# Scaling v of four chunks on VectorE instead of GpSimd, and taking out one group of identity products

## The chip, the cores and the metric

The kernel runs on one core of a Trainium2 chip. The metric is the device time of one execution in microseconds (us), as the median of several runs. The profile is one execution recorded by the hardware; its span, from first to last instruction, is 1.7 us shorter than the time of the same run. In its lines PE is TensorE, PEld TensorE's weight loads, DVE VectorE, ACT ScalarE, POOL GpSimd, and L168 is line 168 of the kernel. A timeline line gives start, duration, engine, line, operation, output from input, and in brackets how long the engine sat idle before it and what ended that; xN means N instructions put into one line. The granted clock is the share of its full speed that TensorE's clock had, as the profile records it.

Each run is on record with a state, fast or slow. All timed runs used below are of the fast state, but for three single runs of the kernel before, whose state is not known; from those only the traces are used.

## The reference

A retention layer (a decaying linear attention, per head h with decay gamma_h) is followed by a gated feed-forward layer:

```
state = gamma[h] * state + outer(k[t], v[t])        # t = 0..767, state 64 x 64
y[t]  = (1/sqrt(64)) * q[t] @ state
x     = y with the 8 heads side by side             # 3072 tokens x 512
out   = (sigmoid(x @ w_gate) * (x @ w_val)) @ w_out # 512 -> 1536 -> 512
```

There are 4 sequences of 768 tokens. The kernel cuts them into 24 chunks of 128 tokens, numbered 0 to 23, six per sequence.

## The kernel before

Each chunk takes these steps: load k, q, v; transpose k and q; scale v by a table of decays (`scale_v`); multiply k and q into scores and mask them; add the part that comes from the state (`inter`) and the part inside the chunk (`intra`); update the state (`state`). Four finished chunks make a tile of 512 tokens for the feed-forward part. The chunk steps of tile t + 1 are placed between the matmuls of tile t. The order of statements is the order in each engine's queue: in the trace of this kernel the last of the twelve loads that the program puts ahead of the scaling of chunk 8 ends on GpSimd at 71.05 us, and the scaling starts at 71.07. In this kernel TensorE's results go to buffers in PSUM, and what the other engines write lies in SBUF. Names in the lines: `kn`, `qn`, `vf` are the loaded k, q, v; `vs` is the scaled v; `tp` the transposes in PSUM and `qkT` their copy (`qkX` where a DMA transposes); `sA`, `sB` the scores; `z` the state; `hT` the gate times the value; `ff` a ring of three PSUM buffers; `tabv`, `taby` the tables of decays. Cuts are marked with `...`.

```python
ld  = ...tile_pool(name="ld", bufs=12)             # k, q: 12 buffers; v: 8; scaled v: 4
pf  = ...tile_pool(name="pf", bufs=3, space=PSUM)  # the ring "ff"
XBAR = 12          # chunks from 12 on are transposed by DMA, those before on TensorE

def load_chunk(g):                                 # three loads issued on GpSimd
    load_kq(g)
    load_v(g, nc.gpsimd)

def scale_v(g, eng):                               # both inputs in SBUF
    vs[g] = ld.tile([C, H, D], BF16, tag="vs", name="vs", bufs=4)
    eng.tensor_tensor(vs[g], vf[g], tabv[...], op=ALU.mult)

def step_t(g):
    if g < XBAR:
        transposes(g)                              # TensorE, then a copy qkT on ScalarE
    scale_v(g, nc.vector if g < 8 else nc.gpsimd)

def keep_on(n):                                    # identity products: results are not used
    u = pf.tile([128, 512], F32, tag="ff", name="ff")
    for _ in range(n):
        nc.tensor.matmul(u[:, :128], ident, ident, start=True, stop=True)

def extend_taby():                                 # "the table product", reads SBUF
    nc.gpsimd.tensor_tensor(taby[:, :, 384:768], taby[:, :, 0:384], ..., op=ALU.mult)
...
    load_gate_val(1); load_gate_val(2)             # weights, in six slices, on GpSimd
    ...
    extend_taby()
    for s in range(3, NFF // 2):
        load_gate_val(s)
    load_chunk(4)
...
    scale_v(3, nc.vector)
    keep_on(8)
    up(0, 0, 0, 384)                               # gate and value matmuls, sigmoid, hT
    up(0, 1, 0, 384)
    transposes(3)
    keep_on(16)
    scores(3)
    masks(3)
    inter(3)
    state(3)
...
for t in range(NT):
    ...
    if t + 2 < NT:
        for g in range(4 * t + 8, 4 * t + 12):     # t = 1: chunks 12 to 15
            load_chunk(g)
    for i, group in enumerate(groups):             # t = 1: step_t(8) to step_t(11) are in here
        group()
        ...
```

In tile 1 the loads of chunks 12 to 15 therefore stand ahead of the scaling of chunks 8 to 11 in GpSimd's queue.

## Time and profile before

| | before |
|---|---|
| time, median of 3 runs | 240.25 us (239.96 to 240.81) |
| profiled run | 239.9 us, span 238.2 us |
| TensorE busy | 229.9 us, 96% |
| TensorE's wait for GpSimd's scaling of chunk 8 | 0.88 us, at 72.18 us |
| wait before the identity products of the fourth chunk | 0.99 us, at 21.17 us |
| VectorE's scaling of v: median and longest | 684 ns, 2307 ns |

TensorE is busy in 96% of the span, and its matmuls run in the order of the program (the scores of the fourth chunk, whose data was there at 21.24 us, start at 22.16, behind the 16 products), so the way to read this kernel is to look for holes in its stream and ask what ended each. The lines are in the prediction below.

### The profile page before, as it was taken

The page shows a single profiled execution, that of the slowest core. Times are in us where ns is not written, and L with a number is a line of the kernel's source. Part 1 is how long each engine was busy: PE and PEld are TensorE (multiplying, and loading weights), DVE is VectorE, ACT ScalarE, POOL GpSimd, SP SyncE. Part 2 cuts the span into 40 slices and gives each one's busy share as a digit, 9 for nine tenths or more (in the row PEclk, how much of TensorE's full clock was granted, in tenths as well). Part 3 has the DMA queues.
Part 4 walks back from the last instruction along what each step waited for, and adds up shares of the span by engine and source line. Part 5 has one row for each costly group of instructions (what it writes and reads, how often), then busy time and mean ns, then how long its engine had stood idle before and what let it go on. Part 6 is the DMA issues. An engine that isn't in the chain of part 4 may idle for free.

```text
span 238.2 us, 4369 instructions
## 1 busy us (share of the span) xinstructions
PE 229.9 (96%) x1754; PEld 120.7 (51%) x1754; DVE 103.0 (43%) x174; ACT 90.8 (38%) x170; POOL 95.9 (40%) x114
## 2 busy tenths in 40 slices
PE   7898999999998999999999999999999999999994
PEld 7665644555654554444554445444445554444443
DVE  3557446355545532166542256641256641234300
ACT  7764334425544442234433234333233431333211
POOL 8999875687889626973411001111000000000000
PEclk9999999999999999999999999999999999999999
DMA  7999999999999999999999462002100011100022
GB/s 136 187 192 183 186 203 204 188 210 223 235 178 128 124 130 160 277 123 120 108 125 152 125 96 44 3 37 80 64 0 0 3 44 73 62 0 0 0 88 88
DMA packets 77699, 27.27 MB, mean 115 GB/s; under 512 B 65072, under 2 KB 73264, under 8 KB 77680
## 3 DMA queue, kind: packets, MB, share of 16 engines
q0 software_dynamic: 57616, 16.78, 71.8%
q1 hardware_dynamic: 19776, 10.10, 22.7%
q8 instruction: 13, 0.21, 0.4%
q10 hardware_dynamic: 288, 0.13, 0.2%
q14 instruction: 6, 0.05, 0.1%
HBM read 28.31 MB, written 6.29 MB: 145 GB/s over the span
## 4 chain that ended last, share of the span: by engine, by line
PE 87%; POOL 7%; issue 2%; DVE 1%; ACT 1%; POOLq 0%; DVEq 0%
PE ff L250 49%; PE ff L281 25%; PE sA L168 3%; PE y L204 2%; PE z L190 2%; POOL kn L67 2%; PE y L180 2%; POOL vf L62 1%; POOL qn L68 1%; POOL vs L158 1%; PE tp L146 1%; PE ff L301 1%; PE ff L264 1%; PE ff L293 1%; DVE xT L212 1%
## 5 line engine op out<-in xcount | busy, mean ns | idle before, releaser
L255 DVE TENSOR_TENSOR hT<-gs,ff 128x512 bf16<-128x512 f32 (+1 forms) x72 | 48.7, 677 | 76.0 <-PE ff L250 74.4
L250 PE MATMUL ff<-xT,wg 128*128 128x512 bf16 (+1 forms) x288 | 72.8, 375 | 0.4 <-DVE xT L212 0.3
L250 PE MATMUL ff<-xT,wv 128*128 128x512 bf16 (+1 forms) x288 | 72.6, 375 | 0.0
L254 ACT ACTIVATE gs<-ff 128x512 f32<-128x512 f32 (+1 forms) x72 | 42.3, 588 | 68.7 <-PE ff L250 68.7
L281 PE MATMUL ff<-wo,hT 128*128 128x512 bf16 x276 | 63.0, 379 | 0.0
L250 PEld LDWEIGHTS <-wv 128*128 128x128 bf16 x288 | 28.2, 98 | 32.7
L250 PEld LDWEIGHTS <-wg 128*128 128x128 bf16 x288 | 26.6, 98 | 30.2 <-issue 0.8
L281 PEld LDWEIGHTS <-hT 128*128 128x128 bf16 x276 | 25.9, 98 | 30.1
L158 POOL TENSOR_TENSOR vs<-vf,tabv 128x512 bf16<-128x512 f32 x18 | 18.6, 1048 | 44.8 <-PE y L204 39.8
L286 ACT COPY ob<-ff 128x512 f32<-128x512 f32 x23 | 13.5, 586 | 52.2 <-PE ff L281 47.0
L62 POOL DMA_DIRECT2D vf<-in_v_dram x23 | 20.7, 898 | 11.5 <-DMA kn<-in_k_dram 6.4
L212 DVE TENSOR_TENSOR xT<-y,taby 128x512 bf16<-128x512 f32 x24 | 16.4, 685 | 20.1 <-PE y L204 20.0
L173 DVE TENSOR_TENSOR stA<-sA,causal 128x512 bf16<-128x512 f32 x24 | 16.5, 687 | 18.7 <-PE sB L168 18.6
L67 POOL DMA_DIRECT2D kn<-in_k_dram x23 | 20.8, 904 | 8.0 <-DMA qn<-in_q_dram 5.7
L68 POOL DMA_DIRECT2D qn<-in_q_dram x23 | 20.4, 886 | 4.0 <-DMA wo<-in_moe_w_out_dram 2.2
L198 ACT CAST zbd<-z 64x256 bf16<-64x256 f32 x40 | 14.7, 366 | 14.5 <-PE z L190 14.1
L174 DVE TENSOR_TENSOR stB<-sB,causal 128x512 bf16<-128x512 f32 x24 | 16.3, 681 | 0.0
L148 ACT ACTIVATE qkT<-tp 128x1024 bf16<-128x1024 bf16 x12 | 12.3, 1025 | 5.1 <-PE tp L146 5.1
L293 PE MATMUL ff<-ident 128*128 128x128 bf16 x110 | 10.0, 257 | 2.6 <-POOL ident masks.py:199 1.6
L293 PEld LDWEIGHTS <-ident 128*128 128x128 bf16 x110 | 8.4, 119 | 3.2 <-POOL ident masks.py:199 1.6
L204 PE MATMUL y<-stA,vs 128*64 128x128 bf16 x96 | 9.7, 222 | 0.0
L204 PE MATMUL y<-stB,vs 128*64 128x128 bf16 x96 | 9.5, 221 | 0.0
(52 smaller groups left out, 119.7 us busy)
## 6 DMA issues: line engine op xcount, KB each, us to landing
vf<-in_v_dram POOLq DMA_DIRECT2D x23, 256.0 KB, 9.2
out_dram<-ob SPq DMA_DIRECT2D x23, 256.0 KB, 2.0
kn<-in_k_dram POOLq DMA_DIRECT2D x23, 128.0 KB, 8.9
qn<-in_q_dram POOLq DMA_DIRECT2D x23, 128.0 KB, 9.2
wg<-in_moe_w_gate_dram POOLq DMA_DIRECT2D x6, 256.0 KB, 5.9
wv<-in_moe_w_val_dram POOLq DMA_DIRECT2D x6, 256.0 KB, 6.6
wo<-in_moe_w_out_dram POOLq DMA_DIRECT2D x4, 384.0 KB, 10.7
kf<-in_k_dram SPq DMA_DIRECT2D x1, 256.0 KB, 3.3
```

What stands on the lines that cost most here:

```text
L62: eng.dma_start(out=vf[g], in_=src(v, g))
L67: nc.gpsimd.dma_start(out=kn[g], in_=src(k, g))
L68: nc.gpsimd.dma_start(out=qn[g], in_=src(q, g))
L158: eng.tensor_tensor(vs[g], vf[g], tabv[:, g % NCH, :].unsqueeze(2).to_broadcast([C, H, D]), op=ALU.mult)
L173: nc.vector.tensor_tensor(stA[g], sc[g][0], causal4, op=ALU.mult)
L204: nc.tensor.matmul(y[g][i * D:(i + 1) * D, p, :], vs[g][:, 2 * p + i, :], st[:, p, :], start=(first and p == 0), stop=True, skip_group_che ...
L212: nc.vector.tensor_tensor(xT[g // 4][:, :, col:col + C], y[g], taby[:, :, c * C:(c + 1) * C], op=ALU.mult)
L250: nc.tensor.matmul(u[:, lo:hi], w[:, kk, n1 * 128:(n1 + 1) * 128], xT[t][:, kk, lo:hi], start=(kk == 0), stop=(kk == KT - 1))
L254: nc.scalar.activation(gs[:, lo:hi], ps[0][:, lo:hi], AX.Sigmoid)
L255: nc.vector.tensor_tensor(hT[t][:, n1, lo:hi], gs[:, lo:hi], ps[1][:, lo:hi], op=ALU.mult)
L281: nc.tensor.matmul(o, hT[t][:, n1, sm * 128:(sm + 1) * 128], wo[:, n1, :], start=(n1 == 0), stop=(n1 == NFF - 1))
L293: nc.tensor.matmul(u[:, :128], ident, ident, start=True, stop=True)
```

## The change

The intent is to remove two delays of TensorE: a group of identity products, and a wait for a scaled v that stands behind twelve load issues.

```diff
     def step_t(g):
         if g < XBAR:
             transposes(g)
-        scale_v(g, nc.vector if g < 8 else nc.gpsimd)
+        scale_v(g, nc.vector if g < XBAR else nc.gpsimd)
@@
     up(0, 1, 0, 384)
     transposes(3)
-    keep_on(16)
     scores(3)
```

The parts are called A (no products) and B (VectorE scales chunks 8 to 11).

## The prediction

> **What bounds the kernel now.** I began with the page: which engine is full, and what the chain that ended last is made of.
>
> ```profile
> PE 229.9 (96%) x1754; PEld 120.7 (51%) x1754; DVE 103.0 (43%) x174; ACT 90.8 (38%) x170; POOL 95.9 (40%) x114
> ...
> PE 87%; POOL 7%; issue 2%; DVE 1%; ACT 1%; POOLq 0%; DVEq 0%
> ```
>
> TensorE (PE) is busy in 96% of a 238.2 us span and holds 87% of the chain. Whatever shortens its in-order stream, or fills a hole in it, comes off the end; work moved between other engines counts only where TensorE waits for it. GpSimd (POOL), 40% busy, holds 7% of the chain, so somewhere TensorE does wait for it. The view of waits of TensorE says how often:
>
> ```profile
> PE z L190 <- POOL vs L158: 1.2, 2, 0.9
> PE ff L293 <- DVE hT L255: 1.0, 1, 1.0
> ```
>
> These are the two waits of weight after the start. The first is one wait of 0.9 us (and one of 0.3 us near 11.7 us, which the change doesn't touch): the state matmuls of a chunk wait for a v scaled on GpSimd. The second is before identity products (line 293). I then read the timeline around each. First the products behind the fourth chunk's transposes:
>
> ```profile
> 17.27 2.82 POOL L130 TENSOR_TENSOR taby<-taby,gup 128x1536 f32<-128x1536 f32 x1
> ...
> 18.35 2.31 DVE L158 TENSOR_TENSOR vs<-vf,tabv 128x512 bf16<-128x512 f32 x1 [1.42 <-DMA vf<-in_v_dram]
> ...
> 20.22 1.02 ACT L148 ACTIVATE qkT<-tp 128x1024 bf16<-128x1024 bf16 x1 [0.61 <-PE tp L146]
> 20.58 1.00 DVE L255 TENSOR_TENSOR hT<-gs,ff 128x384 bf16<-128x384 f32 x2
> 21.17 1.05 PE L293 MATMUL ff<-ident 128*128 128x128 bf16 x16 [0.99 <-DVE hT L255]
> ```
>
> The products write into a PSUM buffer of the ring "ff" (three deep), which comes free only when VectorE has made the first hT. VectorE is late because its scaling of v took 2.31 us beside GpSimd's table product. So the products, meant to fill a hole, begin 0.99 us after TensorE ran dry and end behind it. The data that the next useful work (scores of the fourth chunk) needs was there at 20.22 + 1.02 = 21.24 us; the scores' first row in the same view starts at 22.16.
>
> Then the GpSimd wait, in the timeline of 71 us, with the next chunk's step, which has no wait, below it:
>
> ```profile
> 70.16 0.89 POOL L62 DMA_DIRECT2D vf<-in_v_dram  x1
> ...
> 70.91 0.23 PE L168 MATMUL sA<-qkT 64*128 64x128 bf16 x1
> ...
> 71.07 4.05 POOL L158 TENSOR_TENSOR vs<-vf,tabv 128x512 bf16<-128x512 f32 x4
> ...
> 72.18 0.32 PE L190 MATMUL z<-vs,kn 128*64 128x64 bf16 x8 [0.88 <-POOL vs L158]
> ...
> 78.61 0.23 PE L168 MATMUL sA<-qkT 64*128 64x128 bf16 x1
> ...
> 78.94 0.32 PE L190 MATMUL z<-vs,kn 128*64 128x64 bf16 x8
> ```
>
> GpSimd issues the twelve loads of chunks 12 to 15 before it comes to scaling v of chunk 8, because the program puts those loads ahead in its queue. The last ends at 71.05, the scaling starts at 71.07, TensorE goes on at 72.18. The time of the scaling is set by the loads' queue, not by v, which was issued at 47.18 and landed 7.9 us later, at 55.1.
>
> [...] The scaling has two SBUF inputs. [...] 684 ns in the median of its six VectorE runs, but 2307 ns beside the table product, ending at 20.66, some 0.57 us after the product's end at 20.09. [...]
>
> [...] The trace shows a granted clock of 1.00 in the stretch 20.00 to 21.20, where TensorE worked 0.21 us. No trace here shows what triggers a drop.
>
> [...] The trace says 1042 against 684 ns, a factor of 1.5[...].
>
> **The change part by part.**
>
> Part A, no identity products. It removes 16 matmuls. By duration (219 ns each) they would be 3.5 us, but they are pipelined: 21.17 to 22.16 is 0.99 us for 16, 62 ns each. After it the scores are released by the copy qkT (21.24). At 13.97 us the same step starts 0.06 us after a copy that ended at 13.91, so I put the scores at 21.30. The gain is 22.16 − 21.30 = 0.86 us, not 0.99: 0.13 us of it becomes a wait for ScalarE. The ring of ff buffers turns by one place; the next gate product then needs the first hT (done 21.13) and starts near 22.2, so nothing new binds. VectorE finishes two hT at 21.58, just before the scores can be masked, near 21.73. All that follows moves up by 0.86.
>
> Does that survive up to 71 us? The DMA share is in the nineties, so loads don't move up with TensorE. The tightest is chunk 5: its k was issued at 32.40 and its q at 33.35, both landing 11.1 us later, so 43.5 and 44.45. Its transposes load k at 45.78 and q at 46.16 now, and would at 44.92 and 45.30. That leaves 0.85 us for q. The last piece of the output weights lands near 31.07 + 11.5 = 42.6 and isn't wanted before 44.5. Chunk 6 has k at 46.7 against 48.4. All clear, if narrowly.
>
> Part B, v of chunks 8 to 11 on VectorE. It takes 4 × 1.04 us from GpSimd and adds 4 × 0.68 = 2.7 us to VectorE. For chunk 8 the scaling stands behind an hT row that ends at 61.94; v was there at 55.1, so vs is ready near 62.6 (61.8 with part A), nine us early. The state products then follow the scores as at 78.61 to 78.94, that is by 0.33 us: they would have started at 71.24 instead of 72.18. Gain 0.94 us. VectorE can carry the addition: between two hT rows it waits 1.04 us for TensorE, and one scaling fits; the others fall near 67.6, 77 and 83 us, with v landed at 59.3, 62.6 and 65.8. GpSimd computes nothing then[...].
>
> The parts depend on each other. With A alone, TensorE would arrive 0.86 us earlier at 71 us and wait 0.86 us longer for a GpSimd whose time is set by DMA. B makes A count. Together 0.86 + 0.94 = 1.80 us. After 73 us no wait of TensorE for another engine is above 0.3 us, so the sum should reach the end: 240.25 − 1.80 = 238.45 us.
>
> GpSimd becomes free 4 us earlier and can issue the loads of chunks 16 and 17 from 71 instead of 75 us. But the loads then go at the pace of landings (the rows of chunks 18 and 19 wait 2.2 and 4.2 us for earlier DMAs), so I count nothing. Its next scaling (93.94) is wanted only by 108.5.
>
> **The rivals.**
>
> First, the identity products did a service[...]. For it: they were put there to keep TensorE on. Against: the present trace already has 0.99 us of idleness there with the clock at 1.00, and the hole grows by only 0.13 us. [...] I give it 7%.
>
> Second, part A is lost to late data: TensorE would wait for q of chunk 5 or its kin, as loads stay where they are. For it: margins of 0.85 us with DMA full, and landings that move from run to run. Against: the sum of margins above. The time would be about 239.0 to 239.3. Whatever it waits for there, at least B's 0.94 remains. 12%.
>
> Third, VectorE becomes the late one[...]. For it: the 2.31 us case. Against: v is landed by nine us or more, and no GpSimd arithmetic is left between 55 and 90 us. A block of 1.6 us past a slack of 1 us would cost 0.6 us or so per case. 6%.
>
> Fourth, earlier loads crowd the transposing DMAs of chunks 12 to 15 (issued 66.67 to 83.33, some 10.7 us to land) and the output writes behind them. Against: they are wanted only at 100.83, seven us after. Worth nothing unless they slip by that much. 4%.
>
> **Range and chances.** The centre is 238.45. The three times of before spread over 0.85 us, and my two gains are each good to about 0.2 us if no rival bites. With the rivals, which lean upward, 237.8 to 239.4 should hold it 8 times in 10. Faster by over 2% would need below 235.4, three us more than all I can find; slower by over 2% needs above 245[...]. So 1%, 98%, 1%.
>
> **What would show each step.** In the changed trace: scores of the fourth chunk start near 21.3 us behind the copy qkT, and the wait of line 293 for hT is gone (A). The transposes of chunk 5 start 0.86 us earlier with no wait for a DMA (A carried); if a wait for qn stands there, the second rival is right. The scaling shows ten rows on VectorE, all but one near 684 ns, and fourteen on GpSimd; the state products near 70.4 us follow the scores by 0.33 us and GpSimd leaves the chain between 61 and 72 us (B). Granted clock 1.00 from 20 to 25 us, else the first rival. The span falls from 238.2 to about 236.4. I'd be wrong if the gain is about 0.9 (one part lost), or if a later wait on loads of chunks 12 to 19 stands in TensorE's view.

The trace of the kernel before shows this in their place. VectorE's scaling of v took 684 ns in the median of six, and 2307 ns in the one that ran beside GpSimd's table product; another (at 49.47 us) took 0.68 us beside a load issue of GpSimd from 49.00 to 49.87. The 1042 ns are GpSimd's median for the same scaling. The page's DMA row has a 9 (90% or more) in every slice from 6 to 131 us; in the first trace of the change the load of q of chunk 5 was issued at 33.56 us, against 33.35 before, although TensorE came to its transposes 0.57 us earlier. That landings move from run to run shows in four traces of the kernel before: VectorE's scaling of chunk 3, which waits for its v, started at 18.35, 18.47, 18.41 and 18.45 us. That loads set GpSimd's time at 71 us was inference.

The rivals: the first is that without the products the granted clock falls at the hole. What that would cost was not shown; its 7% was the estimate, from the hole of 0.99 us with the clock at 1.00. The third is that a scaling on VectorE comes late, as the one of 2.31 us did, and delays the hT behind it; its 1.6 us is an estimate, 2307 − 684 ns.

## The result, and the profile after

| | before | after |
|---|---|---|
| median of 4 runs, same rounds | 240.13 us | 238.13 us |
| lowest, highest | 239.96, 240.81 | 238.13, 238.38 |
| span of the profiled run | 238.2 us | 236.7 us |
| granted clock, mean | 1.000 | 0.997 |

The ratio is 0.9914, with a 95% interval of 0.9893 to 0.9935. A ratio here is the mean time of one kernel's fast runs over that of the other's fast runs of the same rounds, so it is not quite the ratio of the medians above. The difference of 2 us is clear of the noise.

The profiled run was the slowest of the four. The other three had a span of 236.4 us. Its extra 0.28 us comes from the start: the first scaling on GpSimd waited for a load of v and began at 8.35 instead of 8.08 us, the second scaling followed it, and from the state products that wait for that one (12.04 instead of 11.75 us) TensorE is later by 0.28. Its clock dips only in the last of 40 slices. A second trace of the changed kernel, taken later, has a span of 236.4 and a start like that of before; it is used beside the first.

The chain that ended last, on the page of the changed kernel. In it GpSimd had 7% before:

```profile
PE 90%; DMA 3%; ACT 2%; POOL 2%; issue 1%; DVE 1%; SPq 0%; ACTq 0%; DVEq 0%; POOLq 0%
```

The waits of TensorE in the changed kernel (total, times, longest):

```profile
PE sA L168 <- ACT qkT L148: 2.1, 4, 1.1
PE ff L293 <- POOL ident masks.py:199: 1.6, 1, 1.6
...
PE z L190 <- POOL vs L158: 0.4, 1, 0.4
```

The wait of line 293 for hT is gone, and so is the 0.88 us at 72 us (the 0.4 left is at 12 us). A wait of 1.1 us for ScalarE's copy qkT has come in; it is the old hole, now ended by the copy. The two places in the timeline of the changed kernel, first the fourth chunk:

```profile
17.54 2.83 POOL L130 TENSOR_TENSOR taby<-taby,gup 128x1536 f32<-128x1536 f32 x1
...
18.14 2.79 DVE L158 TENSOR_TENSOR vs<-vf,tabv 128x512 bf16<-128x512 f32 x1 [0.93 <-DMA vf<-in_v_dram]
...
20.50 1.02 ACT L148 ACTIVATE qkT<-tp 128x1024 bf16<-128x1024 bf16 x1 [0.61 <-PE tp L146]
20.85 1.00 DVE L255 TENSOR_TENSOR hT<-gs,ff 128x384 bf16<-128x384 f32 x2
...
21.58 0.23 PE L168 MATMUL sA<-qkT 64*128 64x128 bf16 x1 [1.12 <-ACT qkT L148]
```

The scores start at 21.58 instead of 22.16 us, 0.58 earlier in a run that was 0.28 late: 0.86 us. Then chunk 8:

```profile
61.28 0.68 DVE L158 TENSOR_TENSOR vs<-vf,tabv 128x512 bf16<-128x512 f32 x1
...
70.33 0.23 PE L168 MATMUL sA<-qkT 64*128 64x128 bf16 x1
...
70.66 0.32 PE L190 MATMUL z<-vs,kn 128*64 128x64 bf16 x8
```

The scaling is done nine us before it is needed, and the state products follow the scores by 0.33 us, as they do in steps without a wait. They start at 70.66 instead of 72.18: with the late start, 1.80 us are gained by here. In the second trace of the change,

```profile
70.39 0.32 PE L190 MATMUL z<-vs,kn 128*64 128x64 bf16 x8
```

that is 1.79 us earlier than before, and the span is 1.8 us shorter. Nothing is lost or won behind this point.

### The profile page after: what moved, and what is told of

It reads as the page before. It is cut to its first block, busy times and chain, and to the rows that moved or that the text cites. A ratio compares the mean times of both kernels' runs of the same rounds, so it can differ in the third digit from the quotient of the medians.

```text
span 236.7 us, 4316 instructions
## 1 busy us (share of the span) xinstructions
PE 227.0 (96%) x1712; PEld 119.5 (51%) x1738; DVE 105.4 (45%) x178; ACT 90.7 (38%) x170; POOL 91.9 (39%) x110
## 4 chain that ended last, share of the span: by engine, by line
PE 90%; DMA 3%; ACT 2%; POOL 2%; issue 1%; DVE 1%; SPq 0%; ACTq 0%; DVEq 0%; POOLq 0%
PE ff L250 51%; PE ff L281 25%; PE sA L168 3%; DMA vf<-in_v_dram 3%; PE y L204 2%; PE y L180 2%; PE z L190 2%; PE tp L146 2%; ACT qkT L148 1%; PE ff L301 1%; POOL vs L158 1%; PE ff L264 1%; DVE xT L212 1%; ACT ob L286 1%; POOL wg L81 0%
## 5 line engine op out<-in xcount | busy, mean ns | idle before, releaser
L250 PE MATMUL ff<-xT,wg 128*128 128x512 bf16 (+1 forms) x276 | 71.5, 375 | 0.9 <-DVE xT L212 0.3
L250 PE MATMUL ff<-xT,wv 128*128 128x512 bf16 (+1 forms) x282 | 71.8, 375 | 0.4
L158 POOL TENSOR_TENSOR vs<-vf,tabv 128x512 bf16<-128x512 f32 x14 | 14.5, 1046 | 44.7 <-PE y L204 39.5
L158 DVE TENSOR_TENSOR vs<-vf,tabv 128x512 bf16<-128x512 f32 x10 | 8.9, 894 | 3.1 <-DMA vf<-in_v_dram 3.1
L293 PE MATMUL ff<-ident 128*128 128x128 bf16 x94 | 8.7, 260 | 1.6 <-POOL ident masks.py:199 1.6
## 6 DMA issues: line engine op xcount, KB each, us to landing
wo<-in_moe_w_out_dram POOLq DMA_DIRECT2D x4, 384.0 KB, 10.4
```

The costliest lines, as they stand in the source:

```text
L158: eng.tensor_tensor(vs[g], vf[g], tabv[:, g % NCH, :].unsqueeze(2).to_broadcast([C, H, D]), op=ALU.mult)
L250: nc.tensor.matmul(u[:, lo:hi], w[:, kk, n1 * 128:(n1 + 1) * 128], xT[t][:, kk, lo:hi], start=(kk == 0), stop=(kk == KT - 1))
```

## The experiments

The kernel before ran beside each set on the same chip. Its own times spread from 238.9 to 241.1 us over these sets, so ratios to it carry an interval of 0.2 to 0.5% either way. The start of single instructions in the traces tells more than the medians, and both are given.

### Each part alone

```diff
# a_only: products out, scaling as before
# b_only: products kept, and
-        scale_v(g, nc.vector if g < 8 else nc.gpsimd)
+        scale_v(g, nc.vector if g < XBAR else nc.gpsimd)
```

> Part A alone: no identity products, v of chunks 8 to 11 still on GpSimd. My theory (the parts depend on each other): the scores of the fourth chunk come 0.86 us earlier, but the state products of chunk 8 still start when GpSimd has scaled v, near 72.2 us, so TensorE's wait there grows from 0.9 to about 1.7 us and the time stays at 240.1 (ratio 0.998 to 1.001). Rival (two independent savings): 239.3, ratio 0.9965, and a wait of 0.9 us as before.

> Part B alone: v of chunks 8 to 11 on VectorE, identity products kept. My theory: 0.94 us less, 239.2, ratio 0.996; no wait of the state products of chunk 8; the products of the fourth chunk still begin 1 us late. Rival (part B does it all, part A is worth nothing): 238.2, ratio 0.992. Second rival (VectorE pays for the scaling): ratio 0.998 to 1.000.

Part A alone took 239.89 us against 240.01 before, ratio 1.0015 (0.9984 to 1.0046). Part B alone took 239.06, ratio 0.9979 (0.995 to 1.0008). The timeline of part A alone, at chunk 8:

```profile
69.97 0.89 POOL L62 DMA_DIRECT2D vf<-in_v_dram  x1
70.87 4.04 POOL L158 TENSOR_TENSOR vs<-vf,tabv 128x512 bf16<-128x512 f32 x4
71.97 0.32 PE L190 MATMUL z<-vs,kn 128*64 128x64 bf16 x8 [1.51 <-POOL vs L158]
```

TensorE had won its 0.84 us by the fourth chunk (scores at 21.32) and gave nearly all of it back here: its wait grew from 0.88 to 1.51 us, and the state products start at 71.97 instead of 72.18. I had expected 1.7; GpSimd came 0.2 us sooner in this run. The rival of two independent savings falls: A is worth nothing measurable while the wait at chunk 8 stands. In B alone the interval of the ratio holds both the expected 0.996 and no gain at all, so the trace has to decide: the state products start 0.93 us earlier than before, behind no wait, and the span is 237.3.

```profile
71.25 0.32 PE L190 MATMUL z<-vs,kn 128*64 128x64 bf16 x8
```

What part A is worth once the wait at chunk 8 is gone shows on the same chip: the version of the next experiment, which has no products and no such wait, took 238.19 us, 0.87 less than part B alone.

### Was it the engine or the place in the queue?

```diff
# queue8: no products; chunk 8 stays on GpSimd, chunks 9 to 11 as before
         for g in range(4 * t + 8, 4 * t + 12):
             load_chunk(g)
+            if g == 12:
+                scale_v(8, nc.gpsimd)
# and step_t(8) no longer scales
```

> Chunk 8 scaled on GpSimd, but put in its queue right behind the loads of chunk 12 in place of behind those of chunk 15; chunks 9 to 11 on GpSimd as before; no identity products. My theory (the place in the queue made the wait, not the engine's speed): as the change, ratio 0.9915 (0.989 to 0.994), the state products of chunk 8 not waiting. Rival (GpSimd's 1.04 against VectorE's 0.68 us, or GpSimd's load as a whole, is what the change removed): some of the wait stays, ratio 0.995 or more.

It took 238.19 us, ratio 0.9935 (0.9913 to 0.9956). Its timeline:

```profile
61.20 1.05 POOL L158 TENSOR_TENSOR vs<-vf,tabv 128x512 bf16<-128x512 f32 x1
...
70.37 0.32 PE L190 MATMUL z<-vs,kn 128*64 128x64 bf16 x8
70.61 3.04 POOL L158 TENSOR_TENSOR vs<-vf,tabv 128x512 bf16<-128x512 f32 x3
```

GpSimd needs 1.05 us where VectorE needs 0.68, and it doesn't matter: done at 62.25, wanted at 70.37. The other three chunks are still scaled behind all the loads and nobody waits for them. So the wait was made by the place in the queue. (Its span is 236.8, 0.4 longer than the change's, with a wait of TensorE of 0.3 us near 97.6 us for an output copy on ScalarE; more of that under the spread of the kernel before.)

### Do the identity products cost time wherever they stand?

```diff
# ontime: the change, with
     transposes(3)
+    keep_on(16)
     scores(3)
# and the table product behind one more slice of weights
+    load_gate_val(3)
     extend_taby()
-    for s in range(3, NFF // 2):
+    for s in range(4, NFF // 2):
# ontime2: the same, behind two more slices (3 and 4)
```

> The change with its 16 identity products put back, and the table product on GpSimd moved behind one more pair of weight loads[...]. My theory (the products cost only because VectorE's lateness pushed them behind the hole): scaling near 0.7 us in place of 2.3 to 2.8, products start near 20.3 us with no wait for hT and end near 21.2, scores near 21.3; ratio 0.9915, as the change. Rival (16 products cost their 1 us wherever they stand): ratio 0.995 to 0.9955, 239.0 us.

That a scaling which starts ahead of the table product isn't slowed by it was the premise.

This failed: 242.01 us, ratio 1.0081 (1.0054 to 1.0109), slower than before. Its timeline shows that the premise did not hold:

```profile
18.54 3.60 DVE L158 TENSOR_TENSOR vs<-vf,tabv 128x512 bf16<-128x512 f32 x1 [1.61 <-DMA vf<-in_v_dram]
18.75 2.83 POOL L130 TENSOR_TENSOR taby<-taby,gup 128x1536 f32<-128x1536 f32 x1
...
22.65 1.42 PE L293 MATMUL ff<-ident 128*128 128x128 bf16 x16 [2.47 <-DVE hT L255]
```

VectorE's scaling has the earlier start, by 0.21 us, and yet it took 3.60 us and ended at 22.14, 0.56 us after GpSimd's product (21.58). It ends 0.57 us after that product in the kernel before and 0.56 in both traces of the change, where the product started first. So the hole before the products grew from 0.99 to 2.47 us. Then the clock fell, as the stretches of this run show (length; busy time and count of PE, PEld, DVE, ACT and POOL; the third number from the end is the granted clock):

```profile
20.00:22.00 2.00, 0.19 (x4) 0.07 (x2) 2.00 (x1) 1.02 (x1) 2.00 (x2) 1.00 1.41 189
22.00:24.00 2.00, 1.35 (x16) 1.15 (x15) 1.06 (x3) 0.00 (x0) 2.00 (x4) 0.80 1.45 198
24.00:26.00 2.00, 2.00 (x23) 1.26 (x23) 1.29 (x2) 0.37 (x2) 1.86 (x3) 0.50 1.46 195
26.00:28.00 2.00, 2.00 (x17) 1.05 (x16) 0.43 (x1) 0.85 (x2) 1.29 (x2) 0.85 1.45 196
```

From about 23.2 to 26.5 us the granted clock was 0.50 (1.00 in the half microsecond before 23.00, 0.91 in the one after 26.50). Five of the six runs had a mean clock of 0.993 and took 242.0; the sixth had 1.000 and took 240.47. The difference, 1.5 us, is what the drop cost here. That run fits the rest without a drop: part B alone takes 239.06, and a hole longer by 2.47 − 0.99 = 1.48 us makes 240.54.

> As the run before with the products put back, but the table product behind two pairs of weight loads, so that it starts near 20 us when VectorE's scaling of chunk 3 (from about 18.5 us, when v has landed) is over. My theory (the 16 products cost only because VectorE's lateness pushed them behind the hole): the scaling takes 0.7 us, the products start near 20.2 with no wait and end near 21.2, scores at 21.3, time as the change (ratio to before 0.991 to 0.994). Rival (the products cost their 1 us wherever they stand): about 239.1, as part B alone.

Here the products stand in the hole: 238.09 us, ratio 0.9942 (0.9916 to 0.9969). Beside it on the same chip the change took 238.09. Its timeline:

```profile
18.73 0.69 DVE L158 TENSOR_TENSOR vs<-vf,tabv 128x512 bf16<-128x512 f32 x1 [1.79 <-DMA vf<-in_v_dram]
19.34 1.07 DVE L255 TENSOR_TENSOR hT<-gs,ff 128x384 bf16<-128x384 f32 x2
20.03 1.06 PE L293 MATMUL ff<-ident 128*128 128x128 bf16 x16
20.20 2.86 POOL L130 TENSOR_TENSOR taby<-taby,gup 128x1536 f32<-128x1536 f32 x1
...
21.31 0.23 PE L168 MATMUL sA<-qkT 64*128 64x128 bf16 x1 [0.22 <-ACT qkT L148]
```

The scores start at 21.31 with the 16 products and at 21.31 without them in the change's second trace. Here the products fill the hole and are free; in the kernel before they cost 0.86 us because VectorE, whose scaling took 2.31 us beside GpSimd's table product where it took 0.69 here, let them start 1 us late. The rival (they cost 1 us wherever they stand) falls.

### The change once more

> The change itself, once more beside the others of this chip. Expected: 238.1, ratio 0.991 to 0.9935.

It took 238.09 us (238.07 to 239.33 in six runs, four of them within 0.02 us), against a median of 239.41 for the kernel before, ratio 0.9953 (0.9925 to 0.9981). The median is where it was; the ratio is worse than expected. The reason is the kernel before, which was faster in this set: three of its eleven runs took 238.93 to 238.95.

### Why the kernel before spreads

Three more traces of the kernel before, unchanged:

> The kernel before, unchanged, to see why its times spread over 2 us while the change repeats to 0.3. My theory: in it TensorE waits for GpSimd behind loads whose landings move from run to run, so the state products of chunk 8 start at the later of 71.24 us and 1.1 us after GpSimd's scaling begins, and the span is that start plus 166.0 us: between 237.3 and 238.6. Rival (the spread comes from the start of the kernel or from elsewhere): the start of the state products minus the start of the scores of chunk 9 does not follow the span.

> As the run before it: span equals the start of the state products of chunk 8 plus 166.0 us.

> As the two runs before it: span equals the start of the state products of chunk 8 plus 166.0 us.

They took 239.42, 239.79 and 239.97 us, single runs whose state is therefore unknown, with granted clocks of 1.000, 0.998 and 1.000. In the first:

```profile
70.58 4.05 POOL L158 TENSOR_TENSOR vs<-vf,tabv 128x512 bf16<-128x512 f32 x4
...
71.70 0.32 PE L190 MATMUL z<-vs,kn 128*64 128x64 bf16 x8 [0.32 <-POOL vs L158]
```

and in the third:

```profile
70.99 4.05 POOL L158 TENSOR_TENSOR vs<-vf,tabv 128x512 bf16<-128x512 f32 x4
72.10 0.32 PE L190 MATMUL z<-vs,kn 128*64 128x64 bf16 x8 [0.86 <-POOL vs L158]
```

The wait at chunk 8 was 0.32, 0.78 and 0.86 us, and 0.88 in the trace of before. The start of these state products against the span, over the traces:

| trace | state products of chunk 8 start at | span | difference |
|---|---|---|---|
| before | 72.18 | 238.2 | 166.0 |
| before, first copy | 71.70 | 237.7 | 166.0 |
| before, second copy | 72.07 | 238.1 | 166.0 |
| before, third copy | 72.10 | 238.3 | 166.2 |
| part A alone | 71.97 | 238.0 | 166.0 |
| part B alone | 71.25 | 237.3 | 166.0 |
| chunk 8 early in GpSimd's queue | 70.37 | 236.8 | 166.4 |
| the change, first trace | 70.66 | 236.7 | 166.0 |
| the change, second trace | 70.39 | 236.4 | 166.0 |

What a kernel has gained or lost by this instruction is nearly all that it ends with. Of the five traces not in the table four give 166.0 as well; the one without products gives 166.9. In the kernel before, the start is set by when GpSimd gets through twelve load issues, and that moves from run to run: its scaling started between 70.58 and 71.07 us. That the landings of earlier loads move it is argued: the profile puts most of GpSimd's short waits between these issues down to VectorE or to nothing, and few to a load (0.48 us in the second copy).

My theory holds, but for three traces in which a later wait adds 0.2, 0.4 and 0.9 us: the third copy, chunk 8 early in GpSimd's queue, and the version without products. All three have the same cause, near 100 us. An output copy on ScalarE waits for an output transfer:

```profile
96.97 0.59 ACT L287 COPY ob<-ff 128x512 f32<-128x512 f32 x1 [4.05 <-DMA out_dram<-ob]
```

This is from the version with chunk 8 early. The copy waited 3.7, 4.1 and 4.6 us in the three, and TensorE waited 0.3 and 0.8 us for it in the last two. In part B alone it waited 3.2 us, which cost nothing; the other traces do not show it.

The theory also says why the gain is not one number: against the first copy the change gains 71.70 − 70.39 = 1.31 us, against the profiled run of before 1.79. Not all of the spread of the kernel before is explained: spans up to 239.4 us occur in its untraced runs, which a wait at chunk 8 of the size seen doesn't reach. The wait for the output transfer could add to it, but no trace shows both large. Nor is all of the spread in the span: two runs of the kernel before took 240.75 and 240.58 us with a span of 238.3, a difference of 2.5 and 2.3 instead of 1.7.

### The next bound

```diff
# early_t: the change, the table product as in ontime2, and
     up(0, 0, 0, 384)
+    transposes(3)
     up(0, 1, 0, 384)
-    transposes(3)
     scores(3)
```

> The change without products, the table product as in the run before it, and the transposes of the fourth chunk between the first two gate-and-value groups in place of behind them, so that ScalarE's copy runs beside matmuls. My theory (the copy is what bounds the scores now, with 1.1 us of hole): scores near 20.05 us, 1.25 us earlier; from there the loads bind, since q of chunk 5 lands near 44.5 and its transposes would want it at 44.05, so TensorE waits some 0.4 us there and 0.85 is left: 237.3. Rival (loads do not bind): 236.9. Rival (the hole is set by something else, the first hT or v): no gain, 238.1.

It took 237.43 us (237.17 to 238.07), ratio 0.9918 (0.9891 to 0.9944), against 238.09 for the change on the same chip: 0.66 us less. It is the fastest version. The scores start at 20.13 instead of 21.31, 1.18 us earlier than in the change's second trace. At 21.95 us TensorE's weight loads wait for a slice of the value weights, which I had not foreseen, and 0.27 us are lost; by the transposes of chunk 5 there are 0.91 us left. There:

```profile
44.02 0.42 PEld L146 LDWEIGHTS <-kn 128*128 128x128 bf16 x4
44.23 0.39 PE L146 MATMUL tp<-ident,kn 128*128 128x128 bf16 x4
44.67 0.23 PEld L146 LDWEIGHTS <-qn 128*128 128x128 bf16 x4 [0.22 <-DMA qn<-in_q_dram]
```

The weights of q would have followed those of k at 44.40 (0.38 us later, as in the kernel before) and waited until 44.67 for the load of q. That costs another 0.27 us where I had expected 0.4. The margin for this load, which the prediction put at 0.85 us, was real: in the change's second trace q landed at about 44.6 and was wanted at 45.31, which leaves 0.7, and 0.91 us earlier was too much for it. Now the loads bind, in two places. The six runs lie between 237.17 and 238.07, where four of six runs of the change on the same chip lay within 0.02 us of each other; that the landings make this spread too is argued, not shown.

### No identity products but those of the start

```diff
# noprod: the change, with every keep_on(n) behind the first, keep_on(36), removed
```

> The change with every later group of identity products taken out too, only the 36 of the start are left. My theory (each of them fills a hole in which TensorE waits for another engine anyway, and the holes stay under 2 us): time as the change, within 0.3 us, if the clock holds. Rival (they keep the clock up): a granted clock below 1.00 between 6 and 24 us and 1.5 us or more on top, 239.6 or later.

It took 243.72 us (243.12 to 244.26), ratio 1.0178 (1.0147 to 1.0208), 5.6 us above the change. My theory falls; the rival's clock is there in the stretches of the profiled run:

```profile
6.00:8.00 2.00, 0.89 (x14) 0.52 (x13) 0.00 (x0) 1.41 (x3) 2.00 (x3) 1.00 1.99 193
8.00:10.00 2.00, 1.42 (x28) 1.00 (x24) 1.29 (x2) 2.00 (x5) 2.00 (x4) 1.00 2.06 158
10.00:12.00 2.00, 1.23 (x20) 0.93 (x20) 1.88 (x3) 0.68 (x3) 2.00 (x3) 0.59 1.24 190
```

It fell to 0.50 near 10.4 us (0.88 in the stretch 10.00 to 10.50, 0.50 in the next) and stayed there until 24 us (0.97 from 24.00 to 24.50), though no single wait listed before it was above 1.1 us (apart from the start). The loss is not the clock's alone. In this trace VectorE's scaling of chunk 2 started at 14.38 and took 3.31 us, beside four load issues of GpSimd and the first 0.41 us of the table product (from 17.28 us), and TensorE waited 2.3 us for it; what slowed it no run settles. Near 103 us TensorE waited 0.8 us for an output copy. One of the five timed runs had a mean clock of 1.000 and still took 243.57, so in that run the time was lost without the clock. There is no trace of it. How the 5.6 us divide between clock and waits stays open. What is shown is that these groups of products may not be taken out together, while the one of the change may.

### All the scaling on VectorE

```diff
-        scale_v(g, nc.vector if g < XBAR else nc.gpsimd)
+        scale_v(g, nc.vector)
```

> The change, with v of all chunks from 8 on scaled on VectorE (12 more instructions of 0.68 us there, 12 of 1.04 us fewer on GpSimd). My theory (neither engine's arithmetic is on the path from there on): 238.1, within 0.3 us of the change. Rival (VectorE pays for added work): 0.5 us or more above it, with waits of TensorE for hT. Rival (GpSimd's arithmetic still delays something): below 237.8.

It took 238.17 us (238.08 to 239.72), ratio 0.9943 (0.9895 to 0.9991), with a span of 236.4. Twelve more instructions on VectorE and twelve fewer on GpSimd change nothing, so neither rival shows here: off the path, this arithmetic costs nothing measurable in either place.

## Why the prediction was right

The measured 238.13 us lie in the range of 237.8 to 239.4, 0.3 us below the centre. By its steps:

**Part A, 0.86 us.** 0.86 in the first trace, 0.85 in the second. The release by the copy qkT is what the profile now names. The reason given for the products' cost is shown by the two versions with the products put back: late by 2.47 us they cost more, in time they cost nothing. In the second the order of the `ff` buffers is that of the kernel before, so that order isn't what part A gained by.

**Carried to chunk 5.** No wait for a load there in the change; the transposes move from 45.99 to 45.15 us in the second trace. The margin called narrow was shown to be so by the version with earlier transposes.

**Part B, 0.94 us.** The state products follow the scores by 0.33 us in both traces. That the queue's order and not the engine made the wait is shown by the run with chunk 8 early in GpSimd's queue.

**A counts only with B.** Part A alone gave 1.0015 and a wait of 1.51 us.

**The sum reaches the end.** 238.2 − 1.80 = 236.4, the span of most runs of the change.

**What was off by 0.3 us.** The steps were read from a run of 239.9 us but taken off the median of 240.25; taken off the profiled run they give 238.1, which is all of the difference. Besides, part B was treated as a fixed 0.94 us, good to 0.2, though the argument itself said that the wait is set by loads: over four traces of the kernel before, the wait at chunk 8 went from 0.32 to 0.88 us. So the size of the gain belongs to the run it was read from, but the end does not: read from the first copy, part B would be 71.70 − 71.25 = 0.45 us, and its span of 237.7 less 0.86 and 0.45 is again 236.4.

**The rivals.** The clock did not drop at the hole of 1.1 us (1.00 in each stretch of 2 us from 18 to 26 in the first trace), as given 93%; in the version whose trace has a hole of 2.47 us it did in five of six runs, and cost 1.5 us. VectorE was not late: the four added rows (at 61.28, 66.99, 75.47 and 82.23 us in the first trace) took 0.68 us each, up to 1.5 us before the times predicted, and the view of line 158 has a median of 682 ns over ten rows with one of 2794, the one beside the table product. GpSimd issued the loads of chunk 16 at 71.56 instead of 75.06 us and nothing came of it.

## What to carry to other kernels

When a full engine waits for a result, look at what stands ahead of that result in the other engine's queue before blaming the other engine's speed; here twelve load issues made the wait, and moving one instruction up would have done as well as changing the engine. An earlier saving on the full engine is worth nothing while a later wait is timed by something else (1.0015 here), so price the two together. Filler work was free here when it started in the hole that it was meant to fill, and cost 0.86 us when it started 1 us late; the other groups of it could not all be taken out. A wait whose length moves from run to run, 0.32 to 0.88 us here, shows itself as a spread of the times.
